# Measured durations and a seeded random search in the list schedule of a linear-attention and MLP kernel

## The chip, the cores and the metric

The kernel runs on one core of a Trainium2 chip. The metric is the device time of one execution in microseconds. Five engines work side by side, each on its own queue of instructions in a fixed order: PE (TensorE, matmuls), ACT (ScalarE), DVE (VectorE), POOL (GpSimd) and SP (SyncE, which here issues every transfer). An instruction starts when it is at the head of its engine's queue and what it reads and writes is free.

## The reference

```
proj = einsum('bhsd,df->bhsf', x, w_phi)                 # for x = q and x = k; 64 -> 128 features
proj = proj - max(abs(proj), over f)
phi(x) = concat(exp(proj), exp(-proj))                   # 256 features
kv  = einsum('bhsf,bhsd->bhfd', phi(k), v);  z = sum over s of phi(k)
out = einsum('bhsf,bhfd->bhsd', phi(q), kv) / (einsum('bhsf,bhf->bhs', phi(q), z) + 1e-6)
x   = out as 4608 tokens x 512
y   = (max(x @ w_in, 0) ** 2) @ w_out                    # 512 -> 2048 -> 512, all float32
```

There are 8 batches, 8 heads, 576 positions and a head size of 64. Two heads make a pair, so there are 32 pairs, four to a batch.

## The kernel before

**Attention.** Pairs 0 to 5 go through `early(p)`, pairs 6 to 31 through `visit(i)` and `late(p)`. In `early`, PE projects the keys (L490, tail L496) and the queries (L605, tail L611) for their maxima, sums keys with values (L546, L551) and the key sums (L578), transposes them (L590), projects the queries again with the maximum subtracted in two halves (L634 and L643), and forms numerators (L660) and denominators (L678). DVE takes maxima (L506, L616) and subtracts (L509), ACT takes the exponentials (keys L512 and L514, queries L650 and L652) and empties accumulators. A denominator goes ACT `sx`, a transfer to `den`, DVE reciprocal `rc`, a transfer to `rd` in DRAM, and a transfer `rb` back that spreads it; then numerator times `rb` (L714) and a split into two float16 halves in the ring of tokens (ACT L733, DVE L736).

**Weights.** `prep` rounds each of eight slices of `w_in` and of `w_out` through ACT (L390, L401), DVE (L393, L397) and POOL (L404). For `w_in` a largest value `wm` follows (ACT L422), spread over the partitions by a PE matmul (L353, in `power`) and made a power of two on DVE (L357 to L361), before `win` is written (ACT L426, DVE L428). For `w_out` follow ACT L435 and POOL L266.

**MLP.** `moe(c, f)` treats 256 tokens (chunk `c`) and 256 hidden features (slice `f`), 18 x 8 steps. A step is 24 matmuls of L912 into a `ph` bank, ReLU and squares on ACT and DVE (L921, L923, L926 or L930, and `gl` at L266), and 12 matmuls of L940 into two `po` banks. Chunk 2 is the first one that needs batch 1, so pairs 4 to 7; chunks 0 and 1 need only pairs 0 to 3.

**Banks.** `pp`, `pn` and `pv` are single accumulators ("single" in the plan): the next user waits until the one before has been read out. `ph` and `po` have two buffers each. Before the MLP starts, the first `BANKS` pairs put their key projection in `po` and their query maxima in `ph`; the pairs from `BANKS` on use `pp` for both. `BANKS` also decides in `tokens` which pairs multiply on POOL (L714) and which on DVE.

**What sets the order.** Every step is an `Op` of a `Plan` with an engine, a duration in us written into the code, the steps that it comes after, the buffers that it uses and a rank. `Plan.order` runs a list schedule: of the steps of an engine that are ready, the lowest rank goes first; for PE a step of another array mode counts 6 us (`STAY`) later. The durations say when a step is ready, so they set the order too. A DVE step with a `lock` is made longer where a POOL step is running. The steps are then written out in the order of their planned starts, and this is the fixed order of each engine. Ranks are in us of the plan: 4.5 per pair, the MLP's matmuls at `LEAD` + step number, the weights at `PREP0` + `PREP1` x number.

Of the kernel before, what the change touches and what calls it, by code (L numbers as in the profile page):

```python
# [45 lines left out]
EARLY = 6  # L46
BANKS = 4
STAY = 6.0
WITH_DVE = 16
CHANGE = 0.15  # L50
RA, RQ, RZ = 1.3, 0.4, 0.3
COLD = 1.12

# [5 lines left out]
WHOLE, ROWS, COLS, STRIPS = range(4)  # L59
# [12 lines left out]
class Plan:  # L72
# [46 lines left out]
    def leads(self, first, op):  # L119
# [9 lines left out]
        return False  # L129

    def order(self):
        for op in self.ops:
            op.next, op.left = [], 0
            op.after = [a for a in {id(a): a for a in op.after}.values() if a is not op]
# [8 lines left out]
        mode = WHOLE  # L143
# [19 lines left out]
        while done < len(self.ops):  # L163
            best = None
# [17 lines left out]
            if taken:  # L182
                parked.setdefault(taken[0], []).append(op)
                continue
            op.start, op.end = t, t + op.us * (COLD if e == "PE" and t < 100.0 else 1.0)
            if op.lock is not None:
# [66 lines left out]
def tile_kernel(ctx, tc, qp, kp, vp, w_phi, w_in, w_out, out):  # L253
# [93 lines left out]
    def power(src, dst, top, after, uses, rank):  # L347
        n = power_n[0]
        power_n[0] += 1
        key = [("pw", n)] + uses  # L350

        def gather():
            PE.matmul(out=pn_["pw", n][:, 0:128], lhsT=src().to_broadcast([128, 128]), rhs=ident, start=True, stop=True)  # L353

        def bits():
            p = pw_[n]
            V.tensor_reduce(out=p[:, 0:1], in_=pn_["pw", n][:, 0:128], op=ALU.max, axis=AX.X)  # L357
            V.tensor_scalar(out=p[:, 1:2].bitcast(I32), in0=p[:, 0:1].bitcast(I32), scalar1=0x7F800000,
                            scalar2=None, op0=ALU.bitwise_and)
            V.tensor_scalar(out=dst[:, 0:1], in0=p[:, 1:2], scalar1=TINY, scalar2=top, op0=ALU.max, op1=ALU.mult)  # L360
            V.reciprocal(out=dst[:, 1:2], in_=dst[:, 0:1])  # L361

        a = P.add("PE", 0.22, gather, after, key + [("pn", ("pw", n))], rank)
        return P.add("DVE", 0.72, bits, [a], key + [("pn", ("pw", n))], rank)

# [4 lines left out]
    def prep(n, f, of_in, rank):  # L370
# [45 lines left out]
        if of_in:  # L416
            cs = slice(256 * f, 256 * f + 256)
            m = cw[:, f, :]
            pm = sm.tile([128, 1], F32, name=f"wm_{f}")

            def most():
                A.activation(out=raw()[:, 0:1024].bitcast(F32), in_=u().bitcast(F32), func=AF.Abs, accum_out=pm)  # L422

            o = raw_read[f] = P.add("ACT", 1.4, most, [o], key, rank)
            o = power(lambda: pm, m, TOP_W, [o], [], rank)
            o = P.add("ACT", 1.1, lambda: A.activation(out=win[0][:, :, cs], in_=value(KT), func=AF.Copy, scale=m[:, 1:2]),  # L426
                      [o], key, rank)
            o = P.add("DVE", 1.27, lambda: V.scalar_tensor_tensor(  # L428
                out=win[1][:, :, cs], in0=value(KT), scalar=m[:, 1:2], in1=win[0][:, :, cs], op0=ALU.mult,
                op1=ALU.subtract), [o], key, rank, lock=4.0)  # L430
        else:
            def high():
                whole = cp.tile([128, 2, 2, DM], F32R, name=f"wout{f}", tag=f"wout{f}")
                wout[f] = [whole[:, i] for i in range(2)]
                A.activation(out=wout[f][0], in_=value(2), func=AF.Copy)  # L435

            o = P.add("ACT", 1.1, high, [o], key, rank)
            o = P.add("POOL", 2.5, lambda: sub(G, wout[f][1], value(2), wout[f][0].bitcast(F32)), [o], key, rank, lock=0.0)
            pool_prep.append(o)
# [117 lines left out]
    def early(p):  # L557
# [6 lines left out]
        k_use = [("po", 2 * p + h) if free else ("pp", ("k", p)) for h in range(2)]  # L564
        km = P.add("PE", 0.96, lambda: k_main(p, k_to), [k_load[p], ld_w], [("k", p)] + k_use, R(0.0), mode=ROWS)
        to_tail = lambda: pn_["k", p][:, 0:128]
# [60 lines left out]
        for c in range(2):  # L627
# [19 lines left out]
            x = 1.3 + 1.5 * c  # L647
            o = P.add("PE", 2.0, q_proj, [q_load[p], minus] + most, [("q", p), pq, ("qm", p)], R(x), mode=(ROWS, WHOLE))
            src = lambda n=n: pp_["q", n][:, :, 0:SH]
# [43 lines left out]
    def denominators(p, dens, rows, rank):  # L693
# [3 lines left out]

        o = P.add("DVE", 0.6, inverse, dens, [("den", p), ("rc", p)], rank, lock=4.0)
        o = P.add("SP", 0.1, lambda: SP.dma_start(rd_[p], rc_[p]), [o], [("rc", p), ("rd", p)], rank, land=2.2)
# [108 lines left out]
    def late(p):  # L808
# [16 lines left out]

        zc = P.add("DVE", 1.2, column, [o], [("z4", p), ("za", p), ("zr", p), ("zc", p)], R(RZ), lock=4.0)
        pq = [("pp", ("Q", p)), ("pn", ("Q", p)), ("pv", ("Q", p))]
# [50 lines left out]
        use = [("d4", p), ("da", p), ("dr", p), ("dt", p)]  # L878
        o = P.add("DVE", 1.3, inverse, dens, use, R(RQ + 1.1), lock=4.0)

# [13 lines left out]
    def moe(c, f, w_done):  # L894
# [20 lines left out]

        g1 = P.add("PE", 2.60, gemm1, after, [("ph", bank)], m)
        if f:
# [17 lines left out]
        def gemm2():  # L935
            for i in range(2):
                for j in range(2):
# [4 lines left out]

        g2 = P.add("PE", 2.87, gemm2, [o] + list(w_done[f, False]),
                   [("gh", n), ("gl", n)] + po, m + 1.5)
# [57 lines left out]
    with tc.manual_schedule():  # L1002
        for op in P.order():
            op.fn()


PREP0, PREP1 = 18.0, 1.0

# [26 lines left out]
```

## Time and profile before

| | us |
|---|---|
| runs, median of 3 (lowest, highest) | 1113.24 (1112.3, 1113.45) |
| the profiled execution's own time | 1108.32 |
| its span, first to last instruction | 1106.5 |
| PE busy in the span | 1071.9 (97%) |
| DVE, ACT, POOL busy | 739.1, 633.5, 183.9 |
| mean granted PE clock | 0.984 |

The span is cut into stages at two points: 112.4 us, where the first L912 starts, and 238.5 us, where chunk 2 starts. Engine rows give start, duration, engine, line, operation, output and inputs, and in brackets how long the engine had been idle before it and what ended that. "issue" there means that the profile shows no releaser. A row that stands for several instructions ends with its count.

### The profile page before, as it was taken

To read this page: it belongs to the slowest core of one execution; us is meant where nothing else is said; L and a number is where in the kernel's file an instruction comes from. 1 tells how busy PE (TensorE), PEld (TensorE's weight loads), DVE (VectorE), ACT (ScalarE), POOL (GpSimd) and SP (SyncE) were. 2 spreads that over 40 slices of the span, in tenths; PEclk is the share of its full clock that TensorE was granted. 3 is DMA by queue.
4 is the path that set the end of the run, shared out by engine and by line. 5 is a ranking of instruction groups with operands and counts; after the bars stand their busy time and mean duration, and the time that the engine had idled before them with its cause. 6 is when DMAs were issued, how large, how long until landed. Compare 5 with 4: busy or idle time off the path is not lost.

```text
span 1106.5 us, 19979 instructions
## 1 busy us (share of the span) xinstructions
PE 1071.9 (97%) x7882; PEld 831.4 (75%) x7882; DVE 739.1 (67%) x1538; ACT 633.5 (57%) x1125; POOL 183.9 (17%) x86
## 2 busy tenths in 40 slices
PE   7868999989999999999999999999999999999998
PEld 5645777767777777777777787777777777888886
DVE  6385988887787888787877687667786875121111
ACT  6787766555656666566665566655554655333332
POOL 1165533111102112111201111110111111000000
PEclk9987999999999999999999999999999999999999
DMA  9733312122122222121221111212111110000000
GB/s 336 266 104 121 104 56 73 55 74 55 55 73 55 73 55 74 55 74 54 74 53 62 36 52 55 74 55 73 43 48 30 36 32 30 11 20 20 1 20 20
DMA packets 68289, 73.50 MB, mean 66 GB/s; under 512 B 36836, under 2 KB 41828, under 8 KB 68196
## 3 DMA queue, kind: packets, MB, share of 16 engines
q1 hardware_dynamic: 68196, 72.23, 21.4%
q8 instruction: 62, 1.02, 0.4%
q14 instruction: 31, 0.25, 0.1%
HBM read 59.18 MB, written 12.99 MB: 65 GB/s over the span
## 4 chain that ended last, share of the span: by engine, by line
PE 74%; DVE 9%; ACT 3%; DMA 3%; issue 2%; POOL 1%; SPq 0%; DVEq 0%; POOLq 0%; ACTq 0%
PE po L940 31%; PE ph L912 29%; PE pv L546 3%; PE pp L833 2%; PE pn L764 2%; PE pp L490 2%; PE pv L764 2%; DMA rb<-rd 1%; PE pv L551 1%; DVE gl L266 1%; DVE pt L860 1%; PE pn L496 1%; DVE qe L266 1%; POOL mx L846 1%; DVE yt L864 1%
## 5 line engine op out<-in xcount | busy, mean ns | idle before, releaser
L912 PE MATMUL ph<-ring,win 128*128 128x256 f16 x3456 | 401.1, 273 | 0.3 <-DVE ring L736 0.3
L912 PEld LDWEIGHTS <-win 128*128 128x128 f16 x3456 | 328.4, 98 | 69.7 <-issue 32.8
L940 PE MATMUL po<-wout,gh 128*128 128x512 f32 x1152 | 371.2, 403 | 0.0
L940 PEld LDWEIGHTS po<-wout,gh 128*128 128x128 f32 x1152 | 207.1, 189 | 47.7 <-issue 5.3
L940 PE MATMUL po<-wout,gl 128*128 128x512 f32 x576 | 227.1, 394 | 3.5 <-DVE gl L266 3.5
L921 ACT ACTIVATE r<-ph,cw 128x512 f32<-128x512 f32 x144 | 98.6, 685 | 223.8 <-PE ph L912 223.4
L846 POOL PARTITION_ALL_REDUCE mx<-pt x52 | 113.8, 2188 | 638.9 <-ACT pt L840 602.6
L266 DVE TENSOR_TENSOR gl<-ph,gh 128x512 fp32r<-128x512 f32 x144 | 98.5, 684 | 158.4 <-ACT ph L930 156.4
L940 PEld LDWEIGHTS po<-wout,gl 128*128 128x128 f32 x576 | 108.6, 189 | 29.1 <-DVE gl L266 4.0
L923 ACT ACTIVATE gh<-r 128x512 fp32r<-128x512 f32 x144 | 90.9, 632 | 4.6
L930 ACT ACTIVATE ph<-r 128x512 f32<-128x512 f32 x128 | 74.7, 583 | 0.0
L786 ACT ACTIVATE n<-pn 128x320 f32<-128x320 f32 x26 | 11.4, 437 | 93.6 <-PE pn L764 93.6
L546 PE MATMUL pv<-e,v 128*64 128x256 f32 x512 | 62.8, 389 | 1.4 <-ACT kz L593 1.4
L266 DVE TENSOR_TENSOR qe<-pt,mx 128x576 f32<-128x576 f32 x52 | 39.3, 755 | 23.0 <-POOL mx L846 22.7
L860 DVE SCALAR_TENSOR_TENSOR pt<-qe,zc,pt 128x576 f32<-128x576 f32 x52 | 42.2, 812 | 12.8 <-ACT pt L858 11.9
L546 PEld LDWEIGHTS pv<-e,v 128*64 128x64 f32 x512 | 36.6, 141 | 18.0 <-issue 2.5
L851 ACT ACTIVATE qe<-qe 128x576 f32<-128x576 f32 x52 | 35.2, 676 | 24.8 <-DVE qe L266 24.6
L512 ACT ACTIVATE e<-e 128x512 f32<-128x512 f32 x64 | 39.7, 621 | 16.1 <-DVE e L509 16.1
L797 DVE STREAM_TRANSPOSE kvs<-pv 128x256 f32<-128x256 f32 x26 | 11.6, 445 | 54.1 <-PE pv L764 48.4
L858 ACT ACTIVATE pt<-qe,zc 128x576 f32<-128x576 f32 x52 | 39.9, 772 | 3.8
L537 DVE TENSOR_TENSOR es<-es,et 64x256 f32<-64x256 f32 x52 | 35.4, 681 | 9.8 <-ACT et L524 8.3
L864 DVE STREAM_TRANSPOSE yt<-pt 128x576 f32<-128x576 f32 x52 | 40.4, 778 | 1.5
(196 smaller groups left out, 1306.4 us busy)
## 6 DMA issues: line engine op xcount, KB each, us to landing
v<-in_vp_dram SPq DMA_DIRECT2D x32, 320.0 KB
k<-in_kp_dram SPq DMA_DIRECT2D x32, 288.0 KB
q<-in_qp_dram SPq DMA_DIRECT2D x32, 288.0 KB
rb<-rd SPq DMA_DIRECT2D x64, 144.0 KB
out_dram<-o SPq DMA_DIRECT2D x36, 256.0 KB
td<-kvs SPq DMA_DIRECT2D x26, 128.0 KB
kz<-td SPq DMA_DIRECT2D x208, 16.0 KB
raw0i<-in_w_in_dram SPq DMA_DIRECT2D x1, 1024.0 KB
```

The lines of the kernel that those rows point to most:

```text
L266: eng.tensor_tensor(out=out_, in0=a, in1=b_, op=ALU.subtract)
L546: PE.matmul(out=to[64 * h:64 * h + 64, 0:256], lhsT=v_[p][:, t, h, :], rhs=e_[2 * p + h][:, t].rearrange("p s f -> p (s f)"), start=t == 0 ...
L764: PE.matmul(out=to[64 * h:64 * h + 64, :], lhsT=kz_[n][:, 128 * s_ + 64 * h:128 * s_ + 64 * h + 64], rhs=qe_[2 * n + h].rearrange("p (s x) ...
L846: o = P.add("POOL", par_us(S), lambda n=n, h=h: G.partition_all_reduce(mx_[n], pt_[p][:, h, :], channels=128, reduce_op=bass_isa.ReduceOp. ...
L858: o = P.add("ACT", act_us(S, 1), lambda h=h, qe=qe, y=y: A.activation(out=y(), in_=qe(0), func=AF.Copy, scale=zc_[p][:, 2 * h:2 * h + 1]), ...
L860: o = P.add("DVE", dve_us(S), lambda h=h, qe=qe, y=y: V.scalar_tensor_tensor(out=y(), in0=qe(1), scalar=zc_[p][:, 2 * h + 1:2 * h + 2], in ...
L864: o = P.add("DVE", dve_us(S), lambda n=n, y=y: V.transpose(yt_["y", n - 2 * EARLY], y()), [o], [("pt", p), ("yt", ("y", n - 2 * EARLY))], ...
L912: PE.matmul(out=ph[:, j, :], lhsT=win[w][:, t, 128 * ff:128 * ff + 128], rhs=ring[half][x][:, t, c0:c0 + T], start=k == 0, stop=k == 3 * K ...
L921: o = P.add("ACT", act_us(512, 1), lambda: A.activation(out=r_[n], in_=ph_[bank], func=AF.Relu, scale=cw[:, f, 0:1]), [g1], [("ph", bank), ...
L923: sq = P.add("ACT", act_us(512), lambda: A.activation(out=gh_[n], in_=r_[n], func=AF.Square), [o], [("r", n), ("gh", n)], Q)
L930: o = P.add("ACT", act_us(512), lambda: A.activation(out=ph_[bank], in_=r_[n], func=AF.Square), [sq], [("ph", bank), ("r", n)], Q)
L940: PE.matmul(out=po_[po[i][1]], lhsT=g[n][:, j, 128 * i:128 * i + 128], rhs=wout[f][w][:, j, :], start=(ff == 0 and s == 0), stop=(ff == 2 ...
```

## The change

The table of durations gets new values; the planner's cold factor is 1.15 instead of 1.12 and holds to 125 us of the plan instead of 100; the weights' ranks start at 16 instead of 18; `BANKS` goes from 4 to 5, so pair 4 uses `po` and `ph` for its projections and POOL for L714; and the list schedule is made 400 times. Each time a twentieth of the steps with ranks between -50 and 70 get a normal shift of 1.5 us, which is kept if the list's end comes no later.

```diff
-BANKS = 4
+BANKS = 5
+TRIALS, SEED, MOVED = 400, 1, 70.0
-COLD = 1.12
+COLD = 1.15
...
+    def improve(self, trials, seed):
+
+        rnd = random.Random(seed)
+        best, plan = None, None
+        some = [op for op in self.ops if -50.0 < op.rank < MOVED]
+        for n in range(trials):
+            moved = rnd.sample(some, len(some) // 20) if n else []
+            old = [(op, op.rank) for op in moved]
+            for op in moved:
+                op.rank += rnd.gauss(0.0, 1.5)
+            order = self.order()
+            length = max(op.end for op in self.ops)
+            if best is None or length <= best:
+                best, plan = length, order
+            else:
+                for op, rank in old:
+                    op.rank = rank
+        return plan
+
     def order(self):
         for op in self.ops:
+            op.start = op.end = None
...
-            op.start, op.end = t, t + op.us * (COLD if e == "PE" and t < 100.0 else 1.0)
+            op.start, op.end = t, t + op.us * (COLD if e == "PE" and t < 125.0 else 1.0)
...
-        zc = P.add("DVE", 1.2, column, [o], [("z4", p), ("za", p), ("zr", p), ("zc", p)], R(RZ), lock=4.0)
+        zc = P.add("DVE", 1.75, column, [o], [("z4", p), ("za", p), ("zr", p), ("zc", p)], R(RZ), lock=4.0)
...
-        o = P.add("DVE", 1.3, inverse, dens, use, R(RQ + 1.1), lock=4.0)
+        o = P.add("DVE", 2.05, inverse, dens, use, R(RQ + 1.1), lock=4.0)
...
-        for op in P.order():
+        for op in P.improve(TRIALS, SEED):
...
-PREP0, PREP1 = 18.0, 1.0
+PREP0, PREP1 = 16.0, 1.0
```

Eight more durations change in the same way: `bits` 0.72 to 0.86, `most` 1.4 to 1.25, `win[1]` 1.27 to 1.5, `k_main` 0.96 to 1.1, `q_proj` of `early` 2.0 to 2.2, `inverse` of `early` 0.6 to 0.45, `gemm1` 2.60 to 2.58, `gemm2` 2.87 to 2.86.

What the change moves is seen in three places. Rows of the changed kernel carry its own line numbers, 22 higher than before from the old L200 on. In a name like `pp_7_800` the 7 counts the uses of `pp`, in `k_4_472` the 4 is the pair; the last number is the program's own, and `...` stands where rows are left out.

First, PE at the projections of pair 4, before:

```order
L353 MATMUL pn_18_823<-ident_72,wm_2_107 128x128
L496 MATMUL pn_19_838<-wraw_76,k_5_576 64x128 x2
L490 MATMUL pp_8_843<-wraw_76,k_4_472 128x128 x8
L605 MATMUL pp_9_883<-wraw_76,q_4_667 128x128 x8
L660 MATMUL pn_20_895<-qe_6_782,kz_3_767 64x288 x4
L546 MATMUL pv_11_904<-e_8_865,v_4_316 64x256
```

and in the changed kernel, from the key projection of pair 4 to the first use of `pp` that comes after pair 3:

```order
L512 MATMUL po_8_752<-wraw_76,k_4_486 128x128
L512 MATMUL po_9_754<-wraw_76,k_4_486 128x128
...
L627 MATMUL ph_8_815<-wraw_76,q_4_676 128x128
L627 MATMUL ph_9_817<-wraw_76,q_4_676 128x128
...
L375 MATMUL pn_18_866<-ident_72,wm_2_107 128x128
L682 MATMUL pv_10_870<-qe_5_697,kz_2_682 64x288 x4
L633 MATMUL pn_19_884<-wraw_76,q_4_676 64x128 x2
L518 MATMUL pn_20_888<-wraw_76,k_5_599 64x128 x2
L568 MATMUL pv_11_897<-e_8_776,v_4_293 64x256
...
L700 MATMUL pn_21_913<-qe_6_831,kz_3_839 32x288
...
L656 MATMUL pp_8_924<-q_4_676,wraw_76 128x288 x2
```

The two projections of pair 4 stood back to back in the one `pp`; now they are in `po` and `ph`, and six steps stand between pair 3's last use of `pp` and the next.

Second, PE at the two halves of pair 4's queries, before:

```order
L634 MATMUL pp_10_976<-q_4_667,wraw_76 128x288 x2
...
L590 MATMUL pv_13_994<-ident_72,kvs_4_965 128x128 x3
L353 MATMUL pn_23_998<-ident_72,wm_3_108 128x128
L634 MATMUL pp_11_1017<-q_4_667,wraw_76 128x288 x2
...
L353 MATMUL pn_24_1032<-ident_72,wm_4_109 128x128
L490 MATMUL pp_12_1041<-wraw_76,k_5_576 128x128 x8
L678 MATMUL pn_25_1060<-qe_8_1000,kz_4_1005 32x288
```

and now:

```order
L656 MATMUL pp_8_924<-q_4_676,wraw_76 128x288 x2
...
L375 MATMUL pn_22_943<-ident_72,wm_3_108 128x128
L573 MATMUL pv_11_897<-et_4_825,v_4_293 64x256 x2
...
L682 MATMUL pn_23_982<-qe_6_831,kz_3_839 64x288 x4
L656 MATMUL pp_9_993<-q_4_676,wraw_76 128x288 x2
...
L612 MATMUL pv_12_1012<-ident_72,kvs_4_991 128x128 x3
L682 MATMUL pv_13_1023<-qe_7_875,kz_3_839 64x288 x4
L512 MATMUL pp_10_1031<-wraw_76,k_5_599 128x128 x8
L700 MATMUL pn_24_1045<-qe_8_972,kz_4_1020 32x288
...
L375 MATMUL pn_25_1067<-ident_72,wm_4_109 128x128
L682 MATMUL pn_26_1080<-qe_8_972,kz_4_1020 64x288 x4
L627 MATMUL pp_11_1090<-wraw_76,q_5_868 128x128 x8
```

Between the halves stood a transpose and one L353; now the rest of pair 4's key sums (L573 and the L600 rows left out) and a numerator stand there. The query maxima of pair 5 are now behind its key projection in `pp`, ahead of the first MLP step.

Third, DVE where chunk 2 begins, before, from the read-out of chunk 1's first output tile (`o_2`) to the last piece of the step after it (`gl_16`):

```order
L951 TENSOR_SCALAR o_2_2542<-po_10_1936,cc_81 128x512
L813 STREAM_TRANSPOSE yt_7_2544<-es_3_2498 128x512
L815 TENSOR_REDUCE z4_3_2547<-yt_7_2544 128x16
L821 COPY za_3_2574<-z4_3_2547 32x16 x4
L822 TENSOR_REDUCE zr_3_2579<-za_3_2574 32x16
L824 COPY zc_3_2581<-zr_3_2579 32x4 x4
L266 TENSOR_TENSOR qe_16_2590<-pt_2_2508,mx_4_2540 128x576
L951 TENSOR_SCALAR o_3_2593<-po_11_1943,cc_81 128x512
L266 TENSOR_TENSOR gl_16_2600<-ph_24_2513,gh_16_2588 128x512
```

and now:

```order
L973 TENSOR_SCALAR o_2_2502<-po_12_1996,cc_81 128x512
L550 TENSOR_TENSOR ez_6_2504<-e_18_2459 128x512
L555 TENSOR_TENSOR es_3_2536<-ez_6_2504 128x256
L559 TENSOR_TENSOR es_3_2536<-es_3_2536,et_9_2485 64x256
L550 TENSOR_TENSOR ez_7_2541<-e_19_2487 128x512
L555 TENSOR_TENSOR es_3_2536<-ez_7_2541 128x256
L973 TENSOR_SCALAR o_3_2576<-po_13_2003,cc_81 128x512
L288 TENSOR_TENSOR gl_16_2580<-ph_26_2506,gh_16_2573 128x512
L288 TENSOR_TENSOR qe_16_2585<-pt_2_2532,mx_4_2543 128x576
```

The key-sum column of pair 9 (L813 to L824) and `qe_16` stood ahead of `gl_16` and now stand behind it; three short sums took part of their place.

More of the change, by code (lines that the diff above doesn't have):

```diff
@@ L1 @@
 import heapq
+import random
 from contextlib import ExitStack
@@ L363, in power @@
         a = P.add("PE", 0.22, gather, after, key + [("pn", ("pw", n))], rank)
-        return P.add("DVE", 0.72, bits, [a], key + [("pn", ("pw", n))], rank)
+        return P.add("DVE", 0.86, bits, [a], key + [("pn", ("pw", n))], rank)
     u_, pool_prep, raw_read = [], [], {}
@@ L422, in most @@
                 A.activation(out=raw()[:, 0:1024].bitcast(F32), in_=u().bitcast(F32), func=AF.Abs, accum_out=pm)
-            o = raw_read[f] = P.add("ACT", 1.4, most, [o], key, rank)
+            o = raw_read[f] = P.add("ACT", 1.25, most, [o], key, rank)
             o = power(lambda: pm, m, TOP_W, [o], [], rank)
@@ L427, in prep @@
                       [o], key, rank)
-            o = P.add("DVE", 1.27, lambda: V.scalar_tensor_tensor(
+            o = P.add("DVE", 1.5, lambda: V.scalar_tensor_tensor(
                 out=win[1][:, :, cs], in0=value(KT), scalar=m[:, 1:2], in1=win[0][:, :, cs], op0=ALU.mult,
@@ L564, in early @@
         k_use = [("po", 2 * p + h) if free else ("pp", ("k", p)) for h in range(2)]
-        km = P.add("PE", 0.96, lambda: k_main(p, k_to), [k_load[p], ld_w], [("k", p)] + k_use, R(0.0), mode=ROWS)
+        km = P.add("PE", 1.1, lambda: k_main(p, k_to), [k_load[p], ld_w], [("k", p)] + k_use, R(0.0), mode=ROWS)
         to_tail = lambda: pn_["k", p][:, 0:128]
@@ L647, in early @@
             x = 1.3 + 1.5 * c
-            o = P.add("PE", 2.0, q_proj, [q_load[p], minus] + most, [("q", p), pq, ("qm", p)], R(x), mode=(ROWS, WHOLE))
+            o = P.add("PE", 2.2, q_proj, [q_load[p], minus] + most, [("q", p), pq, ("qm", p)], R(x), mode=(ROWS, WHOLE))
             src = lambda n=n: pp_["q", n][:, :, 0:SH]
@@ L696, in inverse @@
             V.reciprocal(out=rc_[p], in_=den_[p])
-        o = P.add("DVE", 0.6, inverse, dens, [("den", p), ("rc", p)], rank, lock=4.0)
+        o = P.add("DVE", 0.45, inverse, dens, [("den", p), ("rc", p)], rank, lock=4.0)
         o = P.add("SP", 0.1, lambda: SP.dma_start(rd_[p], rc_[p]), [o], [("rc", p), ("rd", p)], rank, land=2.2)
@@ L914, in gemm1 @@
                         k += 1
-        g1 = P.add("PE", 2.60, gemm1, after, [("ph", bank)], m)
+        g1 = P.add("PE", 2.58, gemm1, after, [("ph", bank)], m)
         if f:
@@ L941, in gemm2 @@
                                   start=(ff == 0 and s == 0), stop=(ff == 2 * NFP - 1 and s == 2))
-        g2 = P.add("PE", 2.87, gemm2, [o] + list(w_done[f, False]),
+        g2 = P.add("PE", 2.86, gemm2, [o] + list(w_done[f, False]),
                    [("gh", n), ("gl", n)] + po, m + 1.5)
```

## The prediction

> **What bounds the kernel now.** I read the page's head first, for the share of PE and the row of granted clocks.
>
> ```profile
> span 1106.5 us, 19979 instructions
> PE 1071.9 (97%) x7882; PEld 831.4 (75%) x7882; DVE 739.1 (67%) x1538; ACT 633.5 (57%) x1125; POOL 183.9 (17%) x86
> PEclk9987999999999999999999999999999999999999
> ```
>
> PE is busy for 97% of the span, and the matmuls themselves stay as they are. So an order can only bring back PE's idle time, 34.6 us, and what PE loses at a low clock. The clock row's 8 and 7 are its third and fourth slices, 55 to 111 us; after that it is hardly below 9. Next I read who PE waits for, up to 140 us (the first seven rows) and after it (the last two); columns are total, times, longest.
>
> ```profile
> PE pp L605 <- issue: 7.3, 1, 7.3
> PE po L490 <- DMA k<-in_kp_dram: 6.2, 2, 4.5
> PE pp L634 <- ACT qe L652: 5.6, 3, 3.3
> PE pv L546 <- ACT kz L593: 1.4, 1, 1.4
> PE pn L660 <- ACT sx L684: 1.4, 1, 1.4
> PE pp L490 <- ACT qe L652: 1.3, 2, 0.8
> PE pn L496 <- DVE pw L357: 0.7, 1, 0.7
> PE po L940 <- DVE gl L266: 3.5, 1, 3.5
> PE ph L912 <- DVE ring L736: 0.3, 1, 0.3
> ```
>
> Nearly all waits that an order could change lie before the first MLP step. After 140 us there is one of size. Busy times by stage follow (window, its length, then PE, weight loads, DVE, ACT, POOL with counts, granted clock, DMA share, GB/s):
>
> ```profile
> 4.50:112.40 107.90, 88.30 (x860) 61.47 (x861) 67.25 (x115) 84.87 (x144) 40.49 (x18) 0.87 0.60 205
> 7.45:115.77 108.32, 88.75 (x869) 61.52 (x869) 69.75 (x120) 88.20 (x149) 41.45 (x19) 0.87 0.57 196
> 112.40:238.50 126.10, 125.54 (x949) 96.33 (x948) 109.72 (x211) 76.94 (x130) 37.99 (x15) 1.00 0.25 73
> 238.50:1106.00 867.50, 858.04 (x6076) 673.64 (x6075) 561.69 (x1209) 470.40 (x852) 105.02 (x48) 1.00 0.17 48
> ```
>
> From 4.5 us, when the first keys land, to the first L912 at 112.4 us, PE is idle for 107.9 - 88.3 = 19.6 us. From 112.4 to 238.5 us it is idle for 0.6 us, and from there to the end for 9.4 us, of which 3.6 us are the wait on `gl` and most of the rest the last read-out and store. What comes earlier at 112.4 us therefore arrives at the end, unless DVE (109.7 of 126.1 us busy there, 87%) or another engine can't follow. That makes four blocks to price, and the question what takes their place.
>
> **The change part by part.** *A, the projections of pair 4.*
>
> ```profile
> 53.44 1.95 PE L546 MATMUL pv<-e,v 128*64 128x256 f32 x16 [1.42 <-ACT kz L593]
> 58.42 1.16 PE L605 MATMUL ph<-wraw,q 64*128 64x128 f32 x16
> 66.93 1.19 PE L660 MATMUL pn<-qe,kz 128*64 128x288 f32 x8
> 74.32 1.22 PE L490 MATMUL pp<-wraw,k 64*128 64x128 f32 x16 [0.76 <-ACT qe L652]
> 82.87 2.08 PE L605 MATMUL pp<-wraw,q 64*128 64x128 f32 x16 [7.33 <-issue]
> 84.88 2.19 PE L660 MATMUL pn<-qe,kz 128*64 128x288 f32 x8
> 86.85 2.94 PE L546 MATMUL pv<-e,v 128*64 128x256 f32 x16
> 82.09 0.67 DVE L509 TENSOR_TENSOR e<-pp,km 128x512 f32<-128x512 f32 x1
> ```
>
> L605 of pair 4 waits 7.33 us behind L490 of the same pair. The page says "issue"; the releaser is the DVE row below, the last reading of `pp`, which ends at 82.76 us, 0.11 us before PE goes on. With five `BANKS` both projections stand in `po` and `ph`, which nobody else uses yet, and six steps stand between the uses of `pp` around them. That takes away 7.33 us and the 0.76 us ahead of L490. Behind the wait the same steps run slow: 2.08 for 1.16 us (L605), 2.19 for 1.19 (L660), 2.94 for 1.95 (L546), together 2.9 us. Block A is 11.0 us, and I put no rest against it here.
>
> *B, the queries of pair 4, and C and D, the smaller waits.*
>
> ```profile
> 39.12 0.76 PE L634 MATMUL pp<-q,wraw 64*128 64x288 f32 x4 [1.64 <-ACT qe L652]
> 99.89 1.33 PE L634 MATMUL pp<-q,wraw 64*128 64x288 f32 x4 [3.29 <-ACT qe L652]
> 106.03 2.08 PE L490 MATMUL pp<-wraw,k 64*128 64x128 f32 x16 [0.56 <-ACT qe L652]
> 111.25 1.19 PE L660 MATMUL pn<-qe,kz 128*64 128x288 f32 x8 [1.38 <-ACT sx L684]
> 112.37 2.79 PE L912 MATMUL ph<-ring,win 128*128 128x256 f16 x24
> 40.00:50.00 10.00, 10.00 (x108) 6.95 (x108) 3.40 (x6) 8.23 (x16) 3.80 (x2) 0.83 0.89 297
> 100.00:110.00 10.00, 9.32 (x50) 6.12 (x50) 4.97 (x8) 7.12 (x10) 6.06 (x3) 0.53 0.57 181
> ```
>
> B: the second half (99.89 us) stands 1 us of PE work behind the first and waits 3.29 us until ACT has taken both exponentials out of `pp`; L490 then waits 0.56 us in the same way. Between 100 and 110 us PE is busy for 9.32 us at a clock of 0.53, so about 9.32 x 0.47 = 4.4 us go to the clock. B is 8.2 us. In the new order the rest of the key sums and a numerator cover the second half.
> C: before 60 us the `qe` row holds 5.6 - 3.3 = 2.3 us, and L546 waits 1.4 us; the clock of 0.83 between 40 and 50 us costs 10 x 0.17 = 1.7 us. C is 5.4 us.
> D: 1.4 us (L660 on `sx`) and 0.7 us (L496 on `pw`), 2.1 us.
>
> [...]
>
> *E, the start of chunk 2.*
>
> ```profile
> 242.80 0.71 PE L940 MATMUL po<-wout,gh 128*128 128x512 f32 x2
> 247.06 0.80 PE L940 MATMUL po<-wout,gl 128*128 128x512 f32 x1 [3.55 <-DVE gl L266]
> 241.02 0.81 DVE L951 TENSOR_SCALAR o<-po,cc 128x512 f32<-128x512 f32 x1
> 246.33 0.68 DVE L266 TENSOR_TENSOR gl<-ph,gh 128x512 fp32r<-128x512 f32 x1
> 238.50:255.00 16.50, 12.71 (x76) 9.79 (x77) 13.29 (x26) 8.06 (x16) 4.69 (x2) 0.79 0.12 47
> ```
>
> PE waits 3.55 us for `gl_16`. DVE has 5.3 us of other work between `o_2` (241.02) and `gl_16` (246.33). Its clock costs 12.71 x 0.21 = 2.7 us, and the wait on the ring 0.3 us: E is 6.5 us. In the new order the column sums and `qe_16` come after `gl_16`, but `o_3` and five sums of key exponentials stand ahead of it. Between nothing and 6.5 us I take half, 3.3 us.
>
> All blocks together: 11.0 + 8.2 + 5.4 + 2.1 + 6.5 = 33.2 us. Against that stand:
>
> - Half of E, 3.2 us.
> - The keys of pair 1, for which PE waits already:
>
> ```profile
> 10.98 2.17 PE L490 MATMUL po<-wraw,k 64*128 64x128 f32 x16 [1.67 <-DMA k<-in_kp_dram]
> ```
>
>   SP now issues `v_1` (320 KB) before `k_1`. At the 297 GB/s of the row for 40 to 50 us that is 1.1 us more wait. L611 of pair 0, moved ahead, is covered by this wait.
> - Short waits on single banks. PE now uses `pn` twice in a row with little between in five places (L611 and L496 of pairs 4 and 5, L353 behind L678, and the like). The waits of 0.56, 0.76 and 0.69 us are the nearest rows: 5 x 0.65 = 3.3 us. Below it is nothing, if ACT and DVE are prompt; above it 5 x 1.64 = 8.2 us.
> - The tail ahead of the first L912. The 1.38 us behind L678 stay. L605 of pair 5 now waits until DVE has read pair 5's keys out of `pp`: four readings at 0.67 us, a power of two and perhaps another step, some 4 us against 2.7 us of PE work between, so 1.3 us; and 1.4 us of clock behind both. Together 4.1 us.
> - New waits between 112 and 238 us, where everything now comes earlier and pair 4's product has gone from DVE to POOL:
>
> ```profile
> 99.36 1.62 SPq L706 DMA_DIRECT2D rb<-rd  x2
> 103.77 1.40 POOL L714 TENSOR_TENSOR rb<-n,rb 128x576 f32<-128x576 f32 x1 [1.47 <-DMA rb<-rd]
> ```
>
>   POOL takes its steps in order and now stands at `rb_4` until a transfer like this one lands, 4.4 us after its issue. The weights' roundings behind it (three at 2.4 us, with ACT between) feed the L353 that PE meets ahead of the third MLP step. I count 1.7 us for this place and as much for one other, 3.5 us. Below it is nothing, since the old trace has only 0.6 us there.
>
> That is 3.2 + 1.1 + 3.3 + 4.1 + 3.5 = 15.2 us, and the gain 33.2 - 15.2 = 18.0 us. Other moves cost nothing: `raw6i`, `v_6` and weights' steps go ahead of `den_0`, which only pair 0 needs, and pair 0's ring is not the last. The last ring that the first L912 needs is pair 3's, whose denominators are these:
>
> ```profile
> 91.48 1.15 PE L678 MATMUL pn<-qe,kz 128*32 128x288 f32 x16
> ```
>
> From the end of this row to the first L912 passed 19.7 us. The new order has about 15 us of PE steps there (twelve, among them both halves of pair 4's queries), so a chain as long as before would make PE wait 4.7 us. I take nothing, because transfers and steps of its own are well under that and the rest was queueing on ACT and DVE; 4.7 us goes into the range. ACT gives an upper bound: from its first work at 7.45 us to the first ReLU at 115.77 us it idles 108.3 - 88.2 = 20.1 us, so the early part can't gain much more than that; blocks A to D less their rests are 18.2 us. From 250 us on the order of MLP steps and visits is nearly the old one, and PE has no idle time to win or cover to lose.
>
> The profiled execution took 1108.3 us, 1.8 us beyond its span; so it becomes 1090.3 us. The median of the runs is 4.9 us above it. With that, 1095 us.
>
> **The rivals.** Changes under 0.2%, 2.2 us, can't be told from none here.
>
> *Given back at chunk 2.* Its first step needs pair 7's ring, which came 0.3 us late already; if DVE, 87% busy, can't bring it forward, PE waits there and half of the 18.2 us is lost: 1104 us. For it speaks that wait, against it that DVE has as many rows done at the first L912 as before (118 to 119) and is rid of one product. Chance 0.15.
>
> *The early waits only move.* The list counts no late transfers and few blocked DVE steps; half of A to D come back as waits on ACT, and E stays: 1107 us. Against it: the cover in the rows around A and B is real work, in order. Chance 0.10.
>
> *Nothing.* If the places I read are only exchanged for others of the same size, 1113 us; chance 0.05.
>
> *Slower.* POOL stands so long at `rb_4` that the weights behind it come late and PE stands at L353 ahead of the third MLP step. A delay of 1.7 us is counted; to outweigh the gain, `rb_4` must land some 20 us later than 4.4 us after its issue, and the clock would fall behind that wait too: 1118 us. SP's queue has nothing long between `rd_4` and `rb_4`, so 0.05.
>
> **How the numbers follow.** The forecast has the remaining 0.65. Its own range is 1088 (no new waits after 112 us and all of E: 18.0 + 3.5 + 3.2 = 24.7 us) to 1101 (the upper end of the single-bank waits, and some of the 4.7 us). The range reaches over the first two rivals to 1107 us and leaves out the last two. Faster by over 0.2%: 0.65 + 0.15 + 0.10 = 0.90; the same 0.05; slower 0.05.
>
> **What would show it.** First L912 at 96 to 98 us instead of 112.4, though PE has then done L605 of pair 5 and one numerator more. No PE wait over 3 us after 12 us. No L605 or L490 of pair 4 on `pp`; the clock near 1.0 between 60 and 90 us. A wait of 1 to 3 us at L605 of pair 5 or the L353 before it. The start of chunk 2 some 17 us earlier and the wait on `gl` shorter. I am wrong if PE waits on `ring` or on L353 for more than 4 us between 100 and 240 us, or if ACT is idle for much more than 8 us before the first ReLU.

## The result, and the profile after

| kernel | runs, median (lowest to highest), us | profiled execution | its span |
|---|---|---|---|
| before | 1112.77 (1108.9 to 1113.45, 4 runs) | 1108.32 | 1106.5 |
| changed | 1087.16 (1085.37 to 1087.31, 4 runs) | 1087.31 | 1085.5 |

The changed kernel takes 0.9773 of the time before, with a 95% interval of 0.9748 to 0.9798. That is 25.6 us by the medians and 21.0 us between the two profiled executions. 1095 us was forecast, with a range of 1088 to 1107: faster, as forecast, but by more, and 0.8 us under the low end.

The head of the page of the changed kernel:

```profile
span 1085.5 us, 19971 instructions
PE 1063.7 (98%) x7882; PEld 826.3 (76%) x7882; DVE 737.3 (68%) x1537; ACT 632.9 (58%) x1125; POOL 185.6 (17%) x87
PEclk9999999999999999999999999999999999999999
```

The 7882 matmuls are the same. PE's busy time fell from 1071.9 to 1063.7 us, 8.2 us, which is the clock (mean granted 0.984 before, 0.997 now), since the work is the same; its idle time fell from 34.6 to 21.8 us, 12.8 us, which is the waits. The 8 and 7 are gone from the clock row. Of 12.8 + 8.2 = 21.0 us, the gain is thus three fifths waits and two fifths clock.

PE's waits of the changed kernel up to 140 us, the three longest (total, times, longest):

```profile
PE po L512 <- DMA k<-in_kp_dram: 4.9, 2, 4.6
PE pn L682 <- DVE et L541: 1.8, 1, 1.8
PE pn L633 <- DVE et L541: 1.6, 1, 1.6
```

And its stages, cut at the first MLP step and at the first matmul of chunk 2:

```profile
4.50:100.60 96.10, 85.32 (x883) 59.00 (x883) 69.18 (x118) 81.34 (x140) 41.22 (x18) 0.98 0.67 230
100.62:223.62 123.00, 121.99 (x916) 94.02 (x914) 108.03 (x207) 79.21 (x134) 39.26 (x16) 1.00 0.25 75
223.62:1085.50 861.88, 856.33 (x6088) 673.29 (x6086) 559.72 (x1209) 471.04 (x852) 104.74 (x48) 1.00 0.17 48
```

The first matmul of chunk 2 starts at 237.19 us in the trace of before (the 238.5 us given ahead of the prediction lie within that step), so the last two stages of before, cut in the same way, are:

```profile
112.37:237.19 124.82, 124.31 (x940) 95.37 (x938) 108.54 (x208) 75.67 (x128) 37.99 (x15) 1.00 0.24 73
237.19:1106.50 869.31, 859.30 (x6087) 674.62 (x6086) 562.90 (x1212) 471.71 (x854) 105.02 (x48) 1.00 0.17 48
```

The 7.3 us at L605 and the 5.6 us at L634 of before are gone, and behind the first load no wait is over 1.9 us. The first MLP step starts at 100.62 instead of 112.37 us, 11.75 us earlier, although two steps of 2.2 us (98.41 to 100.62 us) that stood behind it are now ahead of it: 14.0 us won. Up to chunk 2 the stage takes 123.0 instead of 124.8 us with that work missing, so 0.4 us are lost. From chunk 2 on, 861.9 us stand against 869.3: 7.4 us won, 4.5 of them idle time. 14.0 - 0.4 + 7.4 = 21.0.

The larger waits that are left ahead of the first MLP step, from the rows of PE:

```profile
50.08 1.16 PE L627 MATMUL ph<-wraw,q 64*128 64x128 f32 x16 [0.82 <-DMA q<-in_qp_dram]
...
52.55 1.19 PE L682 MATMUL pn<-qe,kz 128*64 128x288 f32 x8 [1.30 <-ACT sx L706]
...
71.28 1.86 PE L682 MATMUL pn<-qe,kz 128*64 128x288 f32 x8 [1.81 <-DVE et L541]
...
97.24 1.19 PE L682 MATMUL pn<-qe,kz 128*64 128x288 f32 x8 [1.14 <-DVE pw L379]
...
100.62 2.79 PE L934 MATMUL ph<-ring,win 128*128 128x256 f16 x24
```

All but the first of these are waits for the single bank `pn`, as forecast. L627 of pair 5 at 98.41 us, for which 1.3 us were put down, waits for nothing. One sign that was set for being wrong came in part: from 7.45 us to the first ReLU at 103.45 us ACT is idle for 12.3 us, where "much more than 8 us" was named.

### The profile page after: what moved, and what is told of

It reads as the page before. It is cut to its first block, busy times and chain, and to the rows that moved or that the text cites. A ratio compares the mean times of both kernels' runs of the same rounds, so it can differ in the third digit from the quotient of the medians.

```text
span 1085.5 us, 19971 instructions
## 1 busy us (share of the span) xinstructions
PE 1063.7 (98%) x7882; PEld 826.3 (76%) x7882; DVE 737.3 (68%) x1537; ACT 632.9 (58%) x1125; POOL 185.6 (17%) x87
## 3 DMA queue, kind: packets, MB, share of 16 engines
q1 hardware_dynamic: 68196, 72.23, 21.8%
## 4 chain that ended last, share of the span: by engine, by line
PE 88%; DVE 4%; ACT 3%; DMA 2%; issue 1%; POOL 1%; SPq 0%; DVEq 0%; POOLq 0%
PE po L962 35%; PE ph L934 33%; PE pv L568 4%; PE pp L512 3%; PE pn L786 3%; PE pp L855 3%; PE pv L786 2%; PE pv L573 1%; PE pp L665 1%; PE pn L518 1%; DVE u L415 1%; DMA k<-in_kp_dram 1%; DMA den<-sx 1%; ACT u L412 1%; POOL u L426 1%
## 5 line engine op out<-in xcount | busy, mean ns | idle before, releaser
L534 ACT ACTIVATE e<-e 128x512 f32<-128x512 f32 x64 | 39.8, 621 | 21.4 <-DVE e L531 21.2
L536 ACT ACTIVATE e<-e 128x512 f32<-128x512 f32 x64 | 40.2, 629 | 1.7
```

Of the source, the lines that this page charges most:

```text
L536: exps[p].append(P.add("ACT", act_us(512), lambda n=n: A.activation(out=e_[n][:, :, 0, :], in_=e_[n][:, :, 0, :], func=AF.Exp), [o], [("e" ...
```

## The experiments

Ratios are to runs of the kernel before on the same chip; the medians come from several chips, on which the medians of before lay 2 us apart. "The list's own end" is the time at which the kernel's own list schedule puts its last step.

### The parts of the change, alone and in pairs

```diff
e1: -BANKS = 4
    +BANKS = 5
e2: the durations, COLD, its 125 us and PREP0 of the changed kernel; BANKS = 4, TRIALS = 1
e3: e2 with BANKS = 5
e4: -        for op in P.order():
    +        for op in P.improve(400, 1):
e6: the changed kernel with BANKS = 4
e7: e4 with BANKS = 5
```

> Only the fifth PSUM bank of rb is given; durations, ranks and the list without a search are those of before. Theory 1 (the gain is TensorE's waits and the half-clock time that they leave, removed before the first MLP step and at the start of chunk 2, most of it by the new order): the fifth bank alone frees the products but leaves the order that lets the 7.33 us wait at 82.76 and the 3.55 us wait on gl_16 arise, so 2 to 8 us come off, 1104 to 1111 us. Rival (the fifth bank carries the gain, since the waits of before are at bottom waits for a bank): 10 us or more come off, 1102 us or less. A result within 2 us of before would say that the bank gives nothing without the order.

> The durations read from the trace, with the cold-start term, with four banks and without the random search. Theory 1: the order changes at the two places of the gain, so 8 to 16 us come off, 1097 to 1105 us. Rival (the search carries it): the list with better durations alone has the same ranks but for ties, and under 5 us come off, over 1108 us.

> The changed kernel without the 400 trials: durations and fifth bank only. Theory 1: 13 to 22 us come off, 1091 to 1100 us, the wait on gl_16 at the start of chunk 2 gone or under 1 us. Rival (the search carries the gain): 1104 us or more. What is left between this run and the changed kernel's 1087.2 us is the price of the search.

> The search of 400 trials on the old durations and four banks. Theory 1: the search makes a list shorter whose durations are partly wrong, so it gains little that the chip sees, 0 to 8 us, 1105 to 1113 us, and may lose. Rival (any search finds the two places): 10 us or more, 1102 us or less.

> Durations and search, but four banks: only the fifth bank is taken from the changed kernel. The list's own end is 1095.9 us here against 1090.7 with five banks, 1095.2 with the search alone and 1105.7 with durations and five banks but no search. Theory A (the list's end, once it is searched with the better durations, tells the chip's time): 1090 to 1096 us. Theory B (the fifth bank is needed, since pair 4's two projections in one accumulator make TensorE wait whatever stands around them): 1098 us or more, with a wait over 3 us at pair 4's L627 or L656.

> Five banks and search, but the old durations. The list's own end is 1091.8 us, nearly the changed kernel's 1090.7 us. Theory A (the end of a searched list tells the chip's time, whatever the durations): 1087 to 1092 us. Theory C (the search on wrong durations shortens only the list, as it did with four banks, where 3.3 us of list and 7.8 us of time came off): 1096 us or more, with waits of TensorE on DVE's `gl` or `e` that the list doesn't know.

| | bank | durations | search | median, us | ratio (95%) | list's own end |
|---|---|---|---|---|---|---|
| before | | | | 1110.6 to 1112.8 | | 1098.5 |
| e1 | x | | | 1109.86 | 0.9988 (0.9964 to 1.0013) | 1101.2 |
| e2 | | x | | 1109.31 | 0.9977 (0.9956 to 0.9997) | 1103.2 |
| e3 | x | x | | 1104.66 | 0.9922 (0.9896 to 0.9948) | 1105.7 |
| e4 | | | x | 1103.09 | 0.9930 (0.9905 to 0.9955) | 1095.2 |
| e6 | | x | x | 1091.30 | 0.9815 (0.9790 to 0.9839) | 1095.9 |
| e7 | x | | x | 1087.31 | 0.9782 (0.9757 to 0.9806) | 1091.8 |
| changed | x | x | x | 1087.16 | 0.9773 (0.9748 to 0.9798) | 1090.7 |

The column "bank" stands for `BANKS = 5`, which adds no bank (the first expectation has that wrong) but gives pair 4 the use of `po` and `ph`, and POOL its product. By the ratios, the durations alone gave 2.6 us where I expected 8 to 16, and the bank and the durations 8.7 us where I expected 13 to 22; both fell to the rival, that the search carries the gain. The search alone gave 7.8 us, the upper end of what I expected, and the bank alone 1.3 us, within 2 us of before. The bank alone does take away the wait that I called block A. PE's rows of e1:

```profile
87.63 1.16 PE L605 MATMUL pp<-wraw,q 64*128 64x128 f32 x16 [0.17 <-ACT qe L652]
...
107.08 1.33 PE L634 MATMUL pp<-q,wraw 64*128 64x288 f32 x4 [5.86 <-DVE e L509]
...
116.51 2.79 PE L912 MATMUL ph<-ring,win 128*128 128x256 f16 x24
```

L605 (here of pair 5) waits 0.17 us, but 5.86 us come back at a half of the queries, and the first MLP step stands at 116.5 us, later than before. So the wait was exchanged for another. The search is in every version that gains more than 9 us. What the other two parts are worth beside it has no single price: the bank gives 4 us with the new durations (e6 to the changed kernel) and 16 us with the old ones (e4 to e7); the durations give 12 us with four `BANKS` (e4 to e6) and nothing with five, where e7 has the old ones and takes the same time as the changed kernel. Each of these is one order from one seed, and the next part shows how far seeds alone lie apart.

### Is it the search, or this seed?

```diff
-TRIALS, SEED, MOVED = 400, 1, 70.0
+TRIALS, SEED, MOVED = 400, 3, 70.0      (e8; e14: seed 2; e15: seed 4; e16: 4000 trials, seed 1)
```

> The changed kernel with another seed (3); the list's own end is 1091.8 us against 1090.7. Theory A (any search over these durations gives the gain, the end of the list tells it): 1086 to 1091 us. Rival (seed 1 is a lucky one on the chip): 1095 us or more.

> The changed kernel with seed 2; the list's own end is 1095.3 us (seed 1: 1090.7, seed 3: 1091.8, which took 1102.0 us). Theory S (the gain is this seed's order, the list's end tells little between seeds): anywhere from 1087 to 1104 us, and not near 1091 with any certainty. Rival (the list's end tells the time but for an accident with seed 3): 1090 to 1094 us.

> The changed kernel with seed 4; the list's own end is 1095.5 us. Theory S: anywhere from 1087 to 1104 us, at least one of the two new seeds over 1095 us. Rival: 1090 to 1094 us.

> The changed kernel with 4000 trials instead of 400, same seed; the list's own end falls from 1090.7 to 1090.1 us. Rival (a shorter list is a shorter time): 1086 to 1087 us. Theory S (the list has nothing more to tell, and 3600 further shifts exchange the order for another of the same quality by the list): 1085 to 1100 us, more likely slower than the changed kernel than faster.

| | median, us | ratio (95%) | list's own end |
|---|---|---|---|
| seed 1 (the change) | 1087.16 | 0.9773 (0.9748 to 0.9798) | 1090.7 |
| seed 3 (e8) | 1101.97 | 0.9913 (0.9885 to 0.9940) | 1091.8 |
| seed 2 (e14) | 1096.76 | 0.9850 (0.9810 to 0.9890) | 1095.3 |
| seed 4 (e15) | 1093.03 | 0.9821 (0.9782 to 0.9860) | 1095.5 |
| seed 1, 4000 trials (e16) | 1091.62 | 0.9812 (0.9763 to 0.9862) | 1090.1 |

All searched orders are faster than before. But of the 25 us only some 10 come with every one of the four seeds; the rest is this seed's order. And e3 had 8.7 us without any search, so with seed 3 the search added 1 us or nothing (its interval overlaps that of e3). Between seeds the list's end says little: the second shortest is the slowest on the chip, and 4000 trials make the list 0.6 us shorter and bring nothing on the chip (1089.7 to 1093.7 us in four runs). One thing that the list doesn't know shows in seed 3 (start, duration, engine):

```profile
85.55 0.68 DVE L415 TENSOR_SCALAR u<-u 128x1024 int32<-128x1024 int32 x1
...
86.36 3.37 POOL L288 TENSOR_TENSOR wout<-u,wout 128x1024 fp32r<-128x1024 f32 x1 [1.56 <-ACT wout L457]
...
87.40 2.88 DVE L415 TENSOR_SCALAR u<-u 128x1024 int32<-128x1024 int32 x1
...
89.70 2.84 POOL L426 TENSOR_TENSOR u<-u,raw4i 128x1024 int32<-128x1024 int32 x1
...
90.32 3.31 DVE L419 SCALAR_TENSOR_TENSOR u<-raw3o,u 128x1024 int32<-128x1024 int32 x1
...
94.98 0.63 ACT L534 ACTIVATE e<-e 128x512 f32<-128x512 f32 x1 [3.61 <-DVE e L531]
...
97.37 0.79 PE L375 MATMUL pn<-ident,wm 128*128 128x128 f32 x2 [5.45 <-ACT raw4i L444]
```

L415 takes 2.88 us instead of 0.68 and L419 behind it 3.31 us (1.23 at 86.26 us) while POOL runs; ACT stands 3.61 us behind them, and PE 5.45 us behind ACT. The list lengthens L415 for POOL by 0.45 us at most. The trace of the changed kernel has the same: the six L415 that started while POOL was running took 1.46 to 2.94 us, the other ten 0.63 to 0.69 us. In the rows above it is 2.2 us for one step. That this makes up the 15 us between the two seeds is not shown.

### Why the runs gained more than the profiles

```diff
e5:  the changed kernel, nothing edited
e13: the kernel before, nothing edited
e12 (the changed kernel; fill_at[...] is the PE step named, ph_[...] an old tile that nobody reads any more):
+        fills = {fill_at[key].n: (bank, n) for key, bank, n in ((('qt', 4), 7, 4), (('n', 8), 9, 4))}
         for op in P.improve(TRIALS, SEED):
+            bank, n = fills.get(op.n, (0, 0))
+            for i in range(n):
+                PE.matmul(out=flat(ph_[bank])[:, 0:128], lhsT=ident, rhs=ident, start=True, stop=True)
             op.fn()
e9 (the kernel before): the same with ((('k', 4), 7, 4), (('qt', 4), 7, 20), (('q', 9), 7, 10))
```

> The changed kernel once more, unchanged, beside runs of before. It is to tell where the 4.6 us come from by which the runs (25.6 us) gained more than the two profiled executions (21.0 us). Theory 1: before's executions spread over some 10 us (1107.2 to 1116.9 in 27 runs) with waits and half-clock stretches that come and go, and those of the changed kernel don't, so the changed kernel stays within 3 us, 1085 to 1088 us, while before spreads by 6 us or more. Rival: both spread alike, over 6 us, and the four earlier runs of the changed kernel happened to be near each other.

> The kernel before once more, for a second trace. Theory 1 (its spread comes from how its waits fall in the 3.41 us raster of the clock): the same waits at the same steps (over 6 us at L605 of pair 4, about 3 us at its second L634, about 3.5 us on gl_16), but other stretches of low clock, and a span that differs from 1106.5 us by the busy time of TensorE rather than by its idle time. Rival (the waits themselves vary, by transfers or by DVE steps that POOL blocks): the idle times differ by as much as the spans do.

> The kernel before, with idle matmuls (128x128 by 128, their result is never read) put ahead of three waits of pair 4 on TensorE: 4 ahead of L490, 20 ahead of L605, 10 ahead of the second L634. The waits' causes stay; TensorE is only kept busy in them. In ten traces the granted clock falls for whole stretches of 3.41 us on a fixed raster, after a stretch in which TensorE idled for 1.4 us or more. Theory W (waits and clock are two costs, the clock follows from the idle time in a raster stretch): no half clock between 79 and 111 us, the steps behind the waits at full speed (L605 1.16 for 2.08 us, L660 1.19 for 2.19), and 4 to 8 us off: 1103 to 1107 us. Rival (the low clock follows from something else, the power drawn or the DMA traffic, or the steps behind are not what sets the end): the low clock stays and the time is that of before within 2 us.

> The changed kernel with idle matmuls ahead of two of its waits: 4 ahead of L627 of pair 4 (at 50 us) and 4 ahead of the first L682 of pair 4 (at 97 us), the places where the one execution of 1093.1 us lost its clock and that of 1087.3 us didn't. Theory W: all executions at 1085 to 1088 us, none over 1090. Rival (the slow execution came from elsewhere): one or more in ten over 1090 us, as before.

In 106 timed runs, those of e13 among them, the kernel before took 1104.6 to 1119.1 us, with medians of 1110.6 to 1112.8. The changed kernel took 1085.4 to 1087.7 us in seven of eight, and 1093.1 in one. That one fell on the profile, so two traces of one order can be laid side by side. A row of its head, PE's rows at 53 us, and its windows from there (columns as in the stages):

```profile
PE 1069.2 (98%) x7882; PEld 829.1 (76%) x7882; DVE 736.8 (68%) x1537; ACT 633.2 (58%) x1125; POOL 184.5 (17%) x87
```

```profile
50.87 1.16 PE L627 MATMUL ph<-wraw,q 64*128 64x128 f32 x16 [1.95 <-DMA q<-in_qp_dram]
...
53.57 2.19 PE L682 MATMUL pn<-qe,kz 128*64 128x288 f32 x8 [1.54 <-ACT sx L706]
...
61.97 3.68 PE L568 MATMUL pv<-e,v 128*64 128x256 f32 x16 [0.15 <-ACT kz L615]
```

```profile
49.71:53.12 3.41, 1.16 (x16) 0.97 (x16) 2.67 (x2) 1.48 (x4) 1.40 (x1) 1.00 0.40 143
53.12:56.53 3.41, 2.96 (x12) 1.27 (x12) 3.25 (x7) 2.87 (x7) 0.00 (x0) 0.50 0.02 1
56.53:59.95 3.42, 3.42 (x15) 2.43 (x11) 2.74 (x4) 1.94 (x4) 2.08 (x1) 0.50 0.50 135
59.95:63.36 3.41, 3.26 (x15) 2.27 (x17) 2.27 (x6) 1.94 (x3) 0.31 (x1) 0.50 0.11 39
63.36:66.78 3.42, 3.42 (x20) 1.79 (x16) 1.14 (x3) 2.76 (x5) 2.40 (x1) 0.50 0.00 0
```

Its span is 5.8 us longer; PE's busy time accounts for 5.5 of it, its idle time (22.1 us) for 0.3. L627 waited 1.95 us for its queries where it had waited 0.82, PE idled for 2.25 us between 49.71 and 53.12 us, and the clock was half for four stretches of 3.41 us (low stretches from here on). In the trace shown first, the same two waits (0.82 and 1.30 us) fell into two stretches and cost no clock; the one low stretch on its record follows the 1.81 us of idle time ahead of 71.28 us:

```profile
68.25:71.66 3.41, 1.60 (x22) 1.32 (x22) 3.38 (x5) 3.14 (x6) 2.46 (x2) 1.00 0.00 1
71.66:75.07 3.41, 3.41 (x15) 1.61 (x12) 3.41 (x5) 3.18 (x8) 2.73 (x1) 0.50 0.17 48
```

What a low stretch costs can be read from the two traces, since their order is the same. The 53 matmuls that start in the four low stretches keep PE busy for 13.2 us there and for 7.4 us in the trace shown first; 32 more, in two low stretches from 100.92 to 107.74 us, for 6.3 against 3.5 us. That is 8.7 us for six stretches, 1.4 us each. (The low stretch of the trace shown first gives some of it back, which leaves the 5.5 us.)

The second trace of before (span 1109.3 us against 1106.5) has the same large waits, 7.40 us at L605, 3.10 at L634 and 3.29 on `gl`, and as many low stretches on record, ten, at partly other places. Its busy time is 1.5 us longer and its idle time 1.3 us, so the waits vary too: neither theory was all of it. Rows of ACT and PE, the first from the trace of before that the forecast used, the others from the second:

```profile
51.64 0.74 ACT L453 ACTIVATE sx<-v 128x640 bf16<-128x640 f32 x1 [1.54 <-DMA v<-in_vp_dram]
```

```profile
52.11 0.74 ACT L453 ACTIVATE sx<-v 128x640 bf16<-128x640 f32 x1 [2.49 <-DMA v<-in_vp_dram]
...
53.91 3.60 PE L546 MATMUL pv<-e,v 128*64 128x256 f32 x16 [3.75 <-ACT kz L593]
```

L546 waited 1.42 us there and 3.75 us here for `kz`. ACT has L453 of pair 7 ahead of `kz` in its order, and that stands until a transfer lands at about 52 us, whenever PE gets there. In e9 and e10, which leave this place as it is, the wait is 2.41 and 2.6 us, so the first trace has the shortest of the four. Nor is the profiled execution always the faster one: in the 18 experiments it lies between 3.9 us under and 5.8 us over the median of its own runs. So the 4.9 us between that trace and the median were no fixed offset: they are the place of one execution in the spread of a kernel whose waits are long.

The idle matmuls took half of the low stretches away (five left in e9 against ten) but brought 1108.58 us, a ratio of 0.9973 (0.9957 to 0.9989) or 3.0 us, less than Theory W's 4 to 8 us: the four ahead of L490 ran at half clock themselves (0.50 from 75.12 to 78.53 us) and made it late, and in its trace the first MLP step starts at 112.19 us, only 0.2 us earlier than in the first trace of before. What the clock costs apart from the waits is therefore not shown by e9. In e12 all four runs were under 1089.2 us, median 1087.55; with one long run in eight before, four runs can't tell.

### Single moves at the two places where before waits for one step

```diff
e10 (the kernel before; e11: the changed kernel, without the + 1; z_of[9]: the three DVE steps of pair 9's key-sum column):
+        plan = [op for op in plan if op not in z_of[9]]
+        i = plan.index(gl_of[16]) + 1
+        plan[i:i] = z_of[9]
e17 (the kernel before; late: ACT L453 of pair 7 and DVE L458):
+        plan = [op for op in plan if op not in late]
+        i = plan.index(qx_of[4]) + 1        # behind pair 2's first L652
+        plan[i:i] = late
e18: e10 and e17 together
```

> The kernel before, in whose finished list three DVE steps at the start of chunk 2 (pair 9's key-sum column: L813, L815, L821 to L824, 3.0 us) stand behind gl_16 instead of ahead of it. Theory 1 (block E is the wait on `gl` and the clock behind it): the wait of 3.55 us falls to about 0.5 us, no low clock at 246 to 253 us, 3 to 6 us off: 1105 to 1108 us. Rival (what is late next takes its place: the column comes 3 us later, and TensorE waits for what needs it): within 2 us of before, with a new wait between 245 and 300 us.

> The mirror of it: the changed kernel, in whose finished list the same three DVE steps stand directly ahead of gl_16. Theory 1: a wait of about 3 us on `gl` at the start of chunk 2 and one or two stretches of low clock come back, 3 to 6 us more: 1090 to 1093 us. Rival (the wait is covered, since the changed kernel has slack at chunk 2): within 1.5 us of 1087.

> The kernel before, in whose finished list the largest value of pair 7's v (ACT L453, DVE L458, which only batch 1's scale needs) stands behind the exponentials of the queries of pair 2's first half instead of ahead of them and of `kz`. Theory V (the wait of L546 is ACT standing at a transfer for a step that nobody needs yet): the wait of 1.4 to 3.8 us at about 53 us falls under 0.5 us, and the first MLP step comes 1.5 to 4 us earlier, 1107 to 1110 us. Rival (the waits behind take it back, since those at L605 of pair 4 and at its second L634 are set by DVE and ACT): the wait goes, and the time stays within 1 us of before.

> The move of e17 and that of e10 (pair 9's key-sum column behind gl_16) together in the kernel before. Theory V: the gains add up, 3 to 6 us off, 1105 to 1108 us. Rival: no more than the 2.6 us that e10 gave alone.

| | median, us | ratio (95%) |
|---|---|---|
| e10 | 1109.53 | 0.9976 (0.9955 to 0.9998) |
| e17 | 1107.23 | 0.9966 (0.9940 to 0.9992) |
| e18 | 1104.11 | 0.9936 (0.9917 to 0.9956) |
| e11 | 1088.00 | 0.9785 (0.9763 to 0.9808) |

Waits of PE on `gl` at the start of chunk 2, in e10 and then in e11:

```profile
251.10 0.50 PE L946 MATMUL po<-wout,gl 128*128 128x512 f32 x1 [1.52 <-DVE gl L266]
```

```profile
229.77 0.50 PE L968 MATMUL po<-wout,gl 128*128 128x512 f32 x1 [1.61 <-DVE gl L288]
```

In e10 the wait falls from 3.55 to 1.52 us and no low clock follows. It gave 2.7 us by the ratio (0.2 to 5.0), a little under the 3 to 6 us that I expected. In e11 the wait comes back with 1.61 us, without a low stretch, and costs 0.8 us by the medians, within the intervals: under the 3 to 6 us that I expected, nearer to the rival. The changed kernel has slack there that before doesn't have.

e17 removes the wait of L546 altogether; in its trace no wait over 0.3 us is left between 40 and 63 us, and 3.8 us (0.9 to 6.7) come off. Both moves give 7.1 us (4.9 to 9.2), so they add up. In the trace of e18 the wait at L605 is still 6.98 us, and the first MLP step starts at 109.09 us:

```profile
80.04 2.08 PE L609 MATMUL pp<-wraw,q 64*128 64x128 f32 x16 [6.98 <-issue]
...
109.09 2.79 PE L921 MATMUL ph<-ring,win 128*128 128x256 f16 x24
```

No version beat the changed kernel; e7 equals it.

## Why the prediction was right and wrong

Right: that PE's waits and clock before the first MLP step and at chunk 2 carry the gain; that L605 and L490 of pair 4 no longer wait on `pp`; that the waits left are short ones on single banks; that nothing new appears on `ring`, so that what is won early arrives at the end. None of the rivals came: the profile lists no wait of PE at all from 140 us on.

*The offset of 4.9 us was the step that failed: it put the time outside the range.* The sum made 1090.3 us of the profiled execution, which took 1087.3 us; the median of the runs is 1087.2, 0.15 us under it, where 4.9 us above it were counted. The offset was added as if it were the chip's. It belonged to the order of before, whose spread is about 14 us, while seven of the new order's eight runs lie within 2.3 us. Without it, the forecast's own range would have been 1083 to 1096 us.

*Block E and its rest: half of 6.5 us taken, 7.4 us measured.* `o_3` and the five sums that now stand ahead of `gl_16` (five, not the three named ahead of the prediction) don't make it late, and the wait is gone with the clock behind it. The term was mis-sized by 4.1 us; 0.9 us of that is more than the whole block, mostly short waits later on that are gone too.

*New waits between 112 and 238 us: 3.5 us taken, 0.4 us measured.* POOL stands 0.23 us at `rb_4`, and the L375 ahead of the third MLP step waits 0.48 us. An experiment with that product alone on DVE was not run, since there was no wait to explain.

*The early part: 18.2 us taken, 14.0 us measured.* In waits I had 17.7 us less 7.1 of rests, 10.6; measured are 8.8 (19.6 us idle before in 4.50 to 112.37 us, 10.8 after in 4.50 to 100.60). The single-bank waits were more and longer than 5 x 0.65 us: 8.7 us of waits stand between 12 and 100.6 us where I left 6.0, and the keys of pair 1 took 0.9 us less than I had put down. In clock I had 9.0 less 1.4, 7.6; measured are 5.2 (busy 88.3 and 85.3 us, the latter with 2.2 us more work). The prices were nearly right: by the rows, compared with the same steps at full clock, the low stretches of A to C cost 8.5 us, and the new one at 71.66 us costs 1.6. The 1.4 us put down behind the tail's two waits were an estimate for which no row was given: in the trace shown first the clock is 1.00 from 75.07 to 140 us, and in that of 1093.1 us the two low stretches from 100.92 us cost 2.8 us. What the sum left out is the start. The record of the granted clock begins at 13.85 us in the trace of before and at 17.05 us in that of the changed kernel. Ahead of that the views show 1.00, but the rows are at half pace (a first projection of 2.08 us, against 1.16 us later). By those rows, an estimate, this start cost 3.6 us before and 4.8 us after, and 8.5 less 1.6 less 1.2 make 5.7 us, near the 5.2 measured. How long the start stays at half pace varies from execution to execution: in the second one of the kernel before the record begins at 16.34 us.

The errors of chunk 2 and of the new waits, +4.1 and +3.1 us of gain, and that of the early part, -4.2, partly cancelled to the 3 us between 1090.3 us and the profiled execution's 1087.3. That the sum came near was luck in part. And that the durations are measured is not what makes this order good: with the old ones, five `BANKS` and the same seed the search found one as good (e7).

The blocks were not independent either, which the sum took them to be. e1 shows block A's wait going and coming back elsewhere, e13 shows what was won ahead of 52 us lost in the wait for a transfer. That the blocks of the changed kernel did add up is what the search found, and with seed 3 it did not.

## What to carry to other kernels

Before adding an offset between one profiled execution and the median, ask whose it is: here the order with waits of up to 7.4 us spread over 14.5 us, and the one whose waits behind the first load are under 2 us over 2.3 us in seven of eight runs. A random search over a list schedule needs the chip as its judge: lists 1 us apart in length lay 15 us apart in time, and ten times the trials brought nothing. And look in an in-order queue for steps that nobody needs yet standing at a late transfer; moving one such step and the DVE step behind it, without any search, was worth 3.8 us (0.9 to 6.7).

## What the hardware showed unexpectedly

The granted clock changed on a fixed raster in this case. In the 20 traces of this study, up to 260 us, all 42 low stretches that follow the first one of their trace begin a whole number of steps of 3.413 us after it. Of the steps at full clock, from the first record of the clock on, one in which PE idled for 1.8 us or more was followed by half clock in 42 of 42 cases, one with 1.4 to 1.8 us in 12 of 27, and one with less in 8 of 1243. Of 67 low steps in which PE was busy throughout, 54 were followed by full clock and 13 were not. So 1.8 us of idle time, about half a step, were enough each time, even in two pieces: 1.15 and 1.10 us in one step of the execution of 1093.1 us were followed by half clock, while 0.82 and 1.30 us in two steps of that of 1087.3 us were not. Idle time alone does not explain everything: in the trace of before, the step at 37.75 us held 1.37 us of the wait of 1.64 us and the clock fell, while the step at 51.40 us held all of the 1.42 us and it did not. And the clock that the prediction put down to the wait of 7.33 us had fallen at 75.29 us, before that wait began at 75.54 us: ahead of it stand the waits of 0.69 and 0.76 us, and it stayed at 0.50 through the long wait, until 88.95 us. What decides between 0.7 and 1.8 us of idle time stays open.

No trace has a record of the clock for the first 8 to 21 us, and the views show it as 1.00 there. In all 20 the first matmuls ran at half pace (in the traces of before and of the changed kernel the first projection takes 2.08 us, against 1.16 us later), so a stage that includes the start shows too high a clock.
